# Scaled rows at the head of a spectral block: half-width sums in one bank, rows on two engines, warming products on both sides

## The chip, the cores and the metric

The kernel runs on one core of one Trainium2 chip. A core has a matrix engine (TensorE, "PE" in the profile, with its weight loads listed apart as "PEld"), a vector engine (VectorE, "DVE"), a scalar engine (ScalarE, "ACT"), GpSimd ("POOL") and SyncE ("SP"), which here issues nearly all transfers. Each engine works through its own instructions in the order in which they were written; semaphores tie the engines together. The metric is the device time of the whole program in microseconds.

## The reference, cut to what matters

One block of a network, on x of 2048 rows by 512 columns. A vector c gives six modulation rows; the rows of x are normalised, scaled by one plus a modulation row and shifted; a two-dimensional real FFT, a product with complex weights and the inverse FFT mix the whole matrix; then a second normalisation and a Dense–Mish–Dense layer follow, each part added to x through a gate.

```
mod = (_silu(c) @ w_mod).reshape(c.shape[0], 6, 1, -1)
sa, ca, ga, sb, cb, gb = (mod[:, 0], mod[:, 1], mod[:, 2], mod[:, 3], mod[:, 4], mod[:, 5])
h = _layernorm(x, axis=-1) * (1 + ca) + sa
x = x + ga * _A_ref(h, A_w_r, A_w_i)          # rfft2, times w_r + 1j*w_i, irfft2
h = _layernorm(x, axis=-1) * (1 + cb) + sb
x = x + gb * _B_ref(h, B_w1, B_b1, B_w2)      # Dense, Mish, Dense
```

The change concerns the factor `1 + ca` of the first line of h, and the first microseconds of the program around it.

## The kernel before, in words

The FFT is done as products with constant matrices. x is held in 16 tiles of 128 rows by 512 columns (tile n has every 16th row). The first stage, up to about 49 us, takes each tile through two products: along the columns (`p1_row`, line 269, four products whose stationary operand is the tile's turned x, loaded as `xring` from a second copy of x in memory, and whose moving operand is a block of the constant `kr`), and along the rows (`p1_col`, lines 314 to 316, with the constant `mring`, which `p1_split` makes out of the loaded `mraw` by splitting it into a high and a low part on ACT and POOL).

The scale `1 + ca` is not applied to x. It is put into the constant: `krs = kr * (1 + ca)`, one factor for each partition and each of the four blocks j of 128. So before the first row product can begin, `ca` itself has to be worked out: `scale_sums` (line 325) multiplies the four loaded parts k of `wmc` (256 KB each) with `sc`, which is silu(c): 16 products, each with a 128x128 part of `wmc` as the stationary operand and a column of `sc` spread over the moving columns. All moving columns are alike, so each result column holds the same sums, of which `scale_rows` (line 330, DVE) reads one.

The normalisation is applied late as well. `row_sums` multiplies a matrix of ones with `krs`, and ACT copies the result to `kb` (line 280). For tile n, `norm_sums` (lines 183 and 184, DVE) takes mean and variance, `first_guess` (lines 188 and 189, ACT, a logarithm and an exponential) and `first_scale` (line 196, three small DVE instructions) give one over the standard deviation `rstd`, `p1_mean` (line 284, DVE) subtracts mean times `kb` from the row product's result, `p1_cast` (lines 294 to 300, ACT) multiplies with `rstd` and rounds to the high part, and `p1_low` (line 307, DVE) makes the low part. `p1_col` needs both parts.

Every f32 product appears as two matmul records and two weight loads, so that `scale_sums` has 32 of each. `warm` (line 355) is a series of products of ones with ones whose result nobody reads; they keep PE at work while the first transfers are under way. PSUM banks are taken by `bank(tag)`: tags A, B, C and D, two buffers each.

The order of this stage is written out by hand: the engines' orders are those of the calls in the text (the planner's table further down concerns a later stage). SP's queue begins with `sc`, the four parts of `wmc` and `kr`, and goes on with x, turned x and `mraw`, tile by tile.

Of the kernel before, what the change touches and what calls it, by code (L numbers as in the profile page):

```python
# [7 lines left out]
F32 = mybir.dt.float32  # L8
F32R = mybir.dt.float32r
AF = mybir.ActivationFunctionType  # L10
ALU = mybir.AluOpType

P = 128
# [70 lines left out]
def tile_spectral_block(ctx: ExitStack, tc: tile.TileContext, x_d, w1_d, b1_d, w2_d,  # L84
                        c_d, xt_d, wm_d, wq_d, wz_d, kr_d, km_d, kc_d, ki_d, kf_d, kv_d, kw_d, kp_d, out_d):
    nc = tc.nc
# [4 lines left out]
    small = ctx.enter_context(tc.tile_pool(name="small", bufs=4))  # L91
# [21 lines left out]
    def bank(tag):  # L113
        return psum.tile([P, 512], F32, name="bank", tag=tag)
# [8 lines left out]
    def buf(tag, dt=F32):  # L123
        if tag in "ty":
            uses[tag] = uses.get(tag, 1) + 1
            return wide(tag)[:, uses[tag] % 2]
        return work.tile([P, 512], dt, name="buf", tag=tag)

    def plain(t):
        return t.bitcast(F32)  # L130

    x = base.tile([P, N2, D], F32, name="x")
    sc = base.tile([P, 4], F32, name="sc")
# [6 lines left out]
    krs = modr[:, 0].rearrange("p (j e) -> p j e", j=4)  # L140
# [11 lines left out]
    wmc = big.tile([P, 4, 512], F32, name="wmc", tag="cr")  # L152
# [8 lines left out]
    kr = pw.tile([P, 4, P], F32, name="kr")  # L161
# [6 lines left out]
    def scale_spread():  # L168
        ps = bank("D")
        for k in range(4):  # L170
            nc.tensor.matmul(ps[:, k * P:(k + 1) * P], sc[:, k:k + 1].to_broadcast([P, P]), ident,
                             start=True, stop=True)
        st["scb"] = ps
# [7 lines left out]
    def norm_sums(n):  # L181
        t = small.tile([P, 6], F32, name="st")
        nc.vector.bn_stats(t, x[:, n, :])
        nc.vector.bn_aggr(mv[:, n, :], t)
# [6 lines left out]
    def norm_refine(lo, hi, sign, r=None):  # L191
        r = rstd[:, lo:hi] if r is None else r
        t = small.tile([P, 4], F32, name="ve")[:, 0:hi - lo]
        for out, a, one, op in ((t, mv[:, lo:hi, 1], EPS, ALU.add), (t, t, -0.5 * sign, ALU.mult),
                                (rstd[:, lo:hi], t, 1.5 * sign, ALU.add)):
            nc.vector.scalar_tensor_tensor(out, a, one, r, op0=op, op1=ALU.mult)

    def first_guess(lo, hi):
        st["r", lo] = r = bank("D")[:, 0:hi - lo]
        norm_guess(lo, hi, r)  # L200

    def first_scale(lo, hi):
        norm_refine(lo, hi, -1, st.pop(("r", lo)))
# [27 lines left out]
    def load_m(n):  # L231
        nc.sync.dma_start(mraw[:, n, :], km_d[:, n, :])

    def load_x(n):
        nc.sync.dma_start(x[:, n:n + 1, :], xv[:, n:n + 1, :])

    def load_xt(n):
        t = xring[:, n % 8]
        nc.sync.dma_start(t, xt_d[n])
        st["xt", n] = t  # L240

    def load_all(n):
        load_xt(n)
        load_x(n)
        load_m(n)
# [13 lines left out]
    def p1_split(n):  # L259
        m = mt(n)  # L260
        nc.scalar.copy(m[:, 0, 0:256], mraw[:, n, :])
        nc.gpsimd.tensor_tensor(m[:, 1, 0:256], mraw[:, n, :], plain(m[:, 0, 0:256]), op=ALU.subtract)
        nc.gpsimd.tensor_scalar(m[:, :, 256:384], plain(m[:, :, 128:256]), -1.0, 0.0,
                                op0=ALU.mult, op1=ALU.add)

    def row_products(pg, data):
        pgv = pg.rearrange("p (c d q) -> p d c q", c=2, d=4)
        for j in range(4):
            nc.tensor.matmul(pgv[:, j], data(j), krs[:, j, :].rearrange("p (c q) -> p c q", c=2),  # L269
                             start=True, stop=True)  # L270

    def p1_row(n):
        xt = st.pop(("xt", n))
        st["pg", n] = pg = bank("AB"[n % 2])
        row_products(pg, lambda j: xt[:, j, :])

    def row_sums():
        ps = bank("D")
        row_products(ps, lambda j: ones)
        nc.scalar.copy(kb, ps)  # L280

    def p1_mean(n):
        c = st.pop(("pg", n))
        nc.vector.scalar_tensor_tensor(c, kb, mv[:, n, 0:1], c, op0=ALU.mult, op1=ALU.subtract)
        st["c", n] = c

    def p1_cast(n):
        c = st["c", n]
        one = rstd[:, n:n + 1]
        gh, gl = buf("g1", F32R), buf("g2", F32R)  # L290
        if n in POOL_LOW:
            g = buf("t")
            if n == 1:
                nc.scalar.activation(gh, c, AF.Copy, scale=one)
            nc.scalar.activation(g, c, AF.Copy, scale=one)
            if n > 1:
                nc.scalar.copy(gh, g)
            nc.gpsimd.tensor_tensor(gl, g, plain(gh), op=ALU.subtract)
        else:
            nc.scalar.activation(gh, c, AF.Copy, scale=one)  # L300
        st["g", n] = gh, gl
# [17 lines left out]
    def p1_save(n):  # L319
        nc.scalar.copy(a_sb[:, :, n, :], st.pop(("pa", n)).rearrange("p (e q) -> p q e", e=8))  # L320

    def scale_sums(ks, ps):
        for k in ks:
            for j in range(4):
                nc.tensor.matmul(ps[j][:, 0:P], wmc[:, k, j * P:(j + 1) * P], sc[:, k:k + 1].to_broadcast([P, P]),  # L325
                                 start=(k == 0), stop=(k == 3))

    def scale_rows(ps):
        for j in range(4):
            nc.vector.scalar_tensor_tensor(krs[:, j, :], kr[:, j, :], ps[j][:, 0:1], kr[:, j, :],  # L330
                                           op0=ALU.mult, op1=ALU.add)

    def shift_sum(k):
        mod_column(wms[:, k, :], cols[:, 0, 0, k:k + 1], 128.0, bank("D"))
# [17 lines left out]
    def warm(count, tag="B"):  # L352
        ps = bank(tag)
        for _ in range(count):
            nc.tensor.matmul(ps[:, 0:P], ones, ones, start=True, stop=True)

    with tc.manual_schedule():
        nc.sync.dma_start(sc, c_d.rearrange("b (p k) -> p (b k)", k=4))
        nc.scalar.preload_act_table_set("natural_log_exp_and_others")
        for k in range(4):  # L360
            nc.sync.dma_start(wmc[:, k, :], wm_d[1, k])
        nc.sync.dma_start(kr, kr_d)
        load_x(0)
        load_xt(0)
        nc.sync.dma_start(ident, kp_d)
        load_xt(1)
        load_m(0)
        for n in range(1, 8):
            load_x(n)
            if n < 7:  # L370
                load_xt(n + 1)
            load_m(n)
        nc.vector.memset(ones, 1.0)
        nc.vector.memset(eps, EPS)
        nc.vector.memset(b1n[:, NF - 1:NF], 0.0)
        sg = small.tile([P, 4], F32, name="sg")
        nc.scalar.activation(sg, sc, AF.Exp, scale=-1.0)
        nc.vector.tensor_scalar(sg, sg, 1.0, None, op0=ALU.add)
        nc.vector.reciprocal(sg, sg)
        nc.vector.tensor_tensor(sc, sc, sg, op=ALU.mult)  # L380
        warm(6)
        cps = [bank(t) for t in "CCBB"]
        for k in range(4):
            scale_sums((k,), cps)
        scale_rows(cps)
        row_sums()
        norm_sums(0)
        first_guess(0, 1)
        first_scale(0, 1)
        p1_split(0)  # L390
        p1_row(0)
        load_all(8)
        p1_row(1)
        load_all(9)
        scale_spread()
        p1_mean(0)
        p1_cast(0)
        norm_sums(1)
        first_guess(1, 2)
        p1_split(1)  # L400
        nc.scalar.copy(scb, st.pop("scb"))
        p1_low(0)
        p1_mean(1)
        first_scale(1, 2)
        p1_split(2)
        p1_cast(1)
        norm_sums(2)
        for n in range(N2):
            if n >= 1 and n != 2:
                p1_save(n - 1)  # L410
            if n + 2 < N2:
                p1_row(n + 2)
                if n == 2:
                    p1_col(1, range(2, 3))
                    p1_save(1)
                if n + 10 < N2:
                    load_all(n + 10)
                if n == 4:
                    nc.sync.dma_start(wms, wm_d[0].rearrange("k p e -> p k e"))
                if n == 6:  # L420
                    load_rest()
            if 1 <= n and n + 1 < N2:
                p1_mean(n + 1)
                if n % 2:
                    first_scale(n + 1, n + 3)
                p1_cast(n + 1)
            for i in range(n + 2 + (n > 5), min(n + 3 + (n > 4), N2)) if n else ():
                p1_split(i)
            if n:
                p1_low(n)  # L430
            p1_col(n, range(2) if n == 1 else range(3))
            if n + 3 < N2:
                norm_sums(n + 3)
                if n % 2 == 0:
                    first_guess(n + 2, n + 4)
            if 11 <= n < 15:
                shift_sum(n - 11)
        p1_save(N2 - 1)
        shift_rows()
# [846 lines left out]
    start = {}  # L1286
# [232 lines left out]
```

## Time and profile before

| what | value |
| --- | --- |
| median of 3 runs | 367.63 us (367.40 to 367.93) |
| the profiled execution | 368.36 us, of which its span 366.6 us |
| PE busy | 358.6 us (98% of the span) |
| DVE busy | 302.5 us (83%) |
| ACT busy | 266.9 us (73%) |
| POOL busy | 78.3 us (21%) |
| share of the chain that ended last | PE 84%, ACT 5%, DVE 4%, DMA 2% |

Times in rows of the profile count from the start of the span. A row of the timeline has start, duration, engine, line, operation, output and inputs, shapes and a count; in brackets stands the engine's idle time before it with what ended it. A row with a count above one is a group, and its duration reaches from the first start to the last end. Matmul records overlap: the time from one start to the next is less than the duration of one record.

### The profile page before, as it was taken

How to read it: one execution, taken by the hardware profiler on the slowest of the kernel's cores; microseconds unless marked ns; L12 is line 12 of the kernel's file. 1: busy time of each engine (PE TensorE's matmuls, PEld its weight loads, DVE VectorE, ACT ScalarE, POOL GpSimd, SP SyncE). 2: the span in 40 equal slices, each digit the busy share in tenths (PEclk: the TensorE clock that was granted, in tenths of full speed). 3: DMA queues.
4: the chain of work that ended last, by engine and by line, in shares of the span. 5: the costliest groups of instructions: out<-in, count | busy, mean ns of one | idle time of the engine just before them, and what ended most of it. 6: DMA issues, size and time to landing. Idle time of an engine off the chain costs nothing.

```text
span 366.6 us, 7820 instructions
## 1 busy us (share of the span) xinstructions
PE 358.6 (98%) x2666; PEld 333.9 (91%) x2666; DVE 302.5 (83%) x752; ACT 266.9 (73%) x601; POOL 78.3 (21%) x126
## 2 busy tenths in 40 slices
PE   8999999998999999999999999999999999999994
PEld 8999977777999998798999999999999999999994
DVE  1898968888889799998994777998759977887995
ACT  1798879996799999998773878766577753555650
POOL 0588738786011001100002101004100000000000
PEclk9999999999999999999999999999999999999998
DMA  7999997678498776899888877786989678863133
GB/s 254 383 349 377 331 373 250 219 185 305 142 327 254 236 256 230 278 306 322 248 225 292 276 236 200 207 276 206 281 301 243 215 229 266 227 219 62 59 57 115
DMA packets 54343, 89.96 MB, mean 245 GB/s; under 512 B 7552, under 2 KB 20960, under 8 KB 54048
## 3 DMA queue, kind: packets, MB, share of 16 engines
q1 hardware_dynamic: 49728, 74.65, 62.0%
q0 software_dynamic: 2416, 7.87, 9.0%
q10 hardware_dynamic: 2160, 6.95, 6.0%
q8 instruction: 21, 0.34, 0.4%
q14 instruction: 18, 0.15, 0.1%
HBM read 68.21 MB, written 17.57 MB: 234 GB/s over the span
## 4 chain that ended last, share of the span: by engine, by line
PE 84%; ACT 5%; DVE 4%; DMA 2%; POOL 1%; issue 1%; ACTq 1%; SPq 0%; DVEq 0%; POOLq 0%
PE bank L1091 25%; PE bank L991 22%; PE bank L974 6%; PE bank L269 4%; PE bank L869 4%; PE bank L859 3%; PE bank L860 3%; PE bank L1037 3%; PE bank L314 3%; PE bank L1087 3%; DMA hT<-in_B_w_dram 2%; PE bank L1103 2%; PE bank L316 1%; PE bank L315 1%; PE bank L325 1%
## 5 line engine op out<-in xcount | busy, mean ns | idle before, releaser
L991 PE MATMUL bank<-hT,wr 128*128 128x256 f32 x360 | 51.6, 283 | 0.0
L991 PEld LDWEIGHTS bank<-hT,wr 128*128 128x128 f32 x360 | 47.3, 191 | 0.6
L991 PE MATMUL bank<-hB,wr 128*128 128x256 f32 x318 | 46.6, 285 | 0.0
L991 PEld LDWEIGHTS bank<-hB,wr 128*128 128x128 f32 x318 | 41.9, 191 | 0.9
L1143 POOL DMA_DIRECT2D x<-modr x7 | 6.3, 898 | 140.5 <-DVE modr L1142 84.7
L1091 PE MATMUL bank<-w2a,ah 128*128 128x256 f32 x161 | 35.1, 283 | 0.0
L917 DVE TENSOR_TENSOR al<-buf,ah 128x512 fp32r<-128x512 f32 (+1 forms) x45 | 30.1, 668 | 5.7 <-ACT ah L916 4.7
L1091 PE MATMUL bank<-w2b,ah 128*128 128x256 f32 x147 | 32.2, 283 | 0.0
L916 ACT CAST ah<-buf 128x512 fp32r<-128x512 f32 (+1 forms) x45 | 27.0, 602 | 4.5 <-DVE buf L1061 2.6
L1091 PEld LDWEIGHTS bank<-w2a,ah 128*128 128x128 f32 x161 | 27.0, 191 | 0.4
L859 PE MATMUL bank<-kc,d 128*128 128x128 f32 x128 | 24.9, 276 | 0.5 <-ACT d L452 0.5
L1091 PEld LDWEIGHTS bank<-w2b,ah 128*128 128x128 f32 x147 | 24.9, 191 | 0.3
L860 PE MATMUL bank<-kc,d 128*128 128x128 f32 x128 | 24.8, 275 | 0.0
L974 PE MATMUL bank<-hB,wr 128*128 128x512 f32 x96 | 24.4, 393 | 0.0
L1091 PE MATMUL bank<-w,ah 128*128 128x256 f32 x112 | 21.5, 284 | 0.0
L314 PE MATMUL bank<-buf,mring 128*128 128x512 f32 x48 | 20.6, 430 | 0.2 <-DVE buf L307 0.2
L974 PEld LDWEIGHTS bank<-hB,wr 128*128 128x128 f32 x96 | 17.3, 189 | 3.1
L859 PEld LDWEIGHTS bank<-kc,d 128*128 128x128 f32 x128 | 19.4, 192 | 0.7 <-ACT d L452 0.7
L860 PEld LDWEIGHTS bank<-kc,d 128*128 128x128 f32 x128 | 19.5, 192 | 0.0
L1091 PEld LDWEIGHTS bank<-w,ah 128*128 128x128 f32 x112 | 17.7, 191 | 0.6
L608 PEld LDWEIGHTS bank<-kv,a_sb 128*128 128x128 f32 x126 | 15.5, 192 | 2.8 <-issue 2.2
L788 POOL DMA_DIRECT2D turned<-x x16 | 8.9, 568 | 42.1 <-DVE x L782 42.1
(310 smaller groups left out, 1098.2 us busy)
## 6 DMA issues: line engine op xcount, KB each, us to landing
wr<-w_S SPq DMA_DIRECT2D x60, 256.0 KB, 4.0
wr<-w_A SPq DMA_DIRECT2D x45, 256.0 KB, 3.8
w_S<-hT SPq DMA_DIRECT2D x20, 256.0 KB, 2.9
x<-in_A_x_dram SPq DMA_DIRECT2D x16, 256.0 KB, 4.7
xring<-in_x_t_dram SPq DMA_DIRECT2D x16, 256.0 KB, 4.6
w_A<-wr SPq DMA_DIRECT2D x15, 256.0 KB, 3.1
x<-modr POOLq DMA_DIRECT2D x7, 512.0 KB, 5.5
out_dram<-x SPq DMA_DIRECT2D x7, 512.0 KB, 3.8
```

What stands on the lines that cost most here:

```text
L269: nc.tensor.matmul(pgv[:, j], data(j), krs[:, j, :].rearrange("p (c q) -> p c q", c=2), start=True, stop=True)
L314: nc.tensor.matmul(pa, m[:, a, 0:128], g, start=(i == 0), stop=False)
L608: nc.tensor.matmul(pd[:, i * P:(i + 1) * P], y[:, i * P:(i + 1) * P], kv[:, 0:128], start=True, stop=True)
L859: nc.tensor.matmul(o, dj[:, 0:128], kc[0][:, n, :], start=True, stop=False)
L860: nc.tensor.matmul(o, dj[:, 64:192], kc[1][:, n, :], start=False, stop=True)
L869: nc.tensor.matmul(px[:, j * P:(j + 1) * P], e[:, j * P:(j + 1) * P], kiv[:, j, :], start=True, stop=True)
L916: nc.scalar.copy(h, r)
L917: nc.vector.tensor_tensor(l, r, plain(h), op=ALU.subtract)
L974: nc.tensor.matmul(ups[i, t, f], ring[t, a][:, p, b, :], sides[int(a[2]) - 1][:, :, q, b, :], start=(a[2] == "1" and b == 0 and n == 0), s ...
L991: nc.tensor.matmul(o, w[:, p, k, :], h[:, q, k, :], start=(first and n == 0), stop=(last and n == 5), skip_group_check=True)
L1037: nc.tensor.matmul(ups[i, 0][:FL], w1s[:, p, u, :], sides[u // 2][:, :, q, u % 2, :], start=(u == 0 and p + q == 0), stop=(u == 3 and p == ...
L1091: nc.tensor.matmul(out_ps[b][n][:, 256 * half:256 * half + 256], a[p][:, e], w2[t][q][:, r], start=(t == 1 and half == 0 and i == 0), stop ...
```

## The change

`scale_sums` takes one part k at a time and writes all four blocks j into one PSUM bank (columns 0, 128, 256 and 384 on) in place of four banks. Parts 0 and 1 are multiplied with 128 moving columns, parts 2 and 3 with 64. The flag that starts an accumulation stands at the first product of the bank alone.

`scale_rows` first reads the four sums as one strided row and adds 1 (DVE, 128x4), and then scales the four blocks of `kr`, blocks 0 and 2 on DVE and 1 and 3 on ACT. Before, DVE did all four, each straight from PSUM as `kr * ca + kr`.

`warm(6)` becomes `warm(7)`, and a `warm(4)` follows the sums. The row product of tile 0 moves ahead of `row_sums`. `first_scale(0, 1)` moves from before the splitting of `mraw` to behind `p1_mean(0)`. On SP's queue the turned x of tile 0 goes ahead of x of tile 0, `mraw` of tile 0 ahead of the turned x of tile 1, and that ahead of `ident`.

```diff
-    def scale_sums(ks, ps):
-        for k in ks:
-            for j in range(4):
-                nc.tensor.matmul(ps[j][:, 0:P], wmc[:, k, j * P:(j + 1) * P], sc[:, k:k + 1].to_broadcast([P, P]),
-                                 start=(k == 0), stop=(k == 3))
+    def scale_sums(k, ps):
+        for j in range(4):
+            w = 64 if k > 1 else P
+            nc.tensor.matmul(ps[:, P * j:P * j + w], wmc[:, k, j * P:(j + 1) * P], sc[:, k:k + 1].to_broadcast([P, w]),
+                             start=(k == 0 and j == 0), stop=(k == 3), skip_group_check=True)
 
     def scale_rows(ps):
-        for j in range(4):
-            nc.vector.scalar_tensor_tensor(krs[:, j, :], kr[:, j, :], ps[j][:, 0:1], kr[:, j, :],
-                                           op0=ALU.mult, op1=ALU.add)
+        one = small.tile([P, 4], F32, name="one")
+        nc.vector.tensor_scalar(one, ps[:, 0:512:128], 1.0, None, op0=ALU.add)
+        for j in range(0, 4, 2):
+            nc.vector.tensor_scalar(krs[:, j, :], kr[:, j, :], one[:, j:j + 1], None, op0=ALU.mult)
+            nc.scalar.activation(krs[:, j + 1, :], kr[:, j + 1, :], AF.Copy, scale=one[:, j + 1:j + 2])
...
         nc.sync.dma_start(kr, kr_d)
+        load_xt(0)
         load_x(0)
-        load_xt(0)
+        load_m(0)
+        load_xt(1)
         nc.sync.dma_start(ident, kp_d)
-        load_xt(1)
-        load_m(0)
...
-        warm(6)
-        cps = [bank(t) for t in "CCBB"]
+        warm(7)
+        cps = bank("C")
         for k in range(4):
-            scale_sums((k,), cps)
+            scale_sums(k, cps)
+        warm(4)
         scale_rows(cps)
+        p1_row(0)
         row_sums()
         norm_sums(0)
         first_guess(0, 1)
-        first_scale(0, 1)
         p1_split(0)
-        p1_row(0)
         load_all(8)
         p1_row(1)
         load_all(9)
         scale_spread()
         p1_mean(0)
+        first_scale(0, 1)
         p1_cast(0)
```

PE, the head of the program before (`modr,ones` is `row_sums`, `modr,xring` the row product of a tile, line 171 a spreading of `sc` that is needed later, line 314 the start of tile 0's `p1_col`; the count is of products):

```order
L355 MATMUL bank<-ones 128x128 x6
L325 MATMUL bank<-sc,wmc 128x128 x16
L269 MATMUL bank<-modr,ones 128x2x64 x4
L269 MATMUL bank<-modr,xring 128x2x64 x8
L171 MATMUL bank<-ident,sc 128x128 x4
L269 MATMUL bank<-modr,xring 128x2x64 x4
L314 MATMUL bank<-buf,mring 128x512
```

The same place of PE in the changed kernel:

```order
L357 MATMUL bank<-ones 128x128 x7
L325 MATMUL bank<-sc,wmc 128x128 x8
L325 MATMUL bank<-sc,wmc 128x64 x8
L357 MATMUL bank<-ones 128x128 x4
L269 MATMUL bank<-modr,xring 128x2x64 x4
L269 MATMUL bank<-modr,ones 128x2x64 x4
L269 MATMUL bank<-modr,xring 128x2x64 x4
L171 MATMUL bank<-ident,sc 128x128 x4
L269 MATMUL bank<-modr,xring 128x2x64 x4
L314 MATMUL bank<-buf,mring 128x512
```

Between the last of the sums and `row_sums` there was nothing; now four warming products and tile 0's row product stand there.

DVE from the scaling of the rows on, before (`BN_STATS` and `BN_AGGR` are `norm_sums`, of tile 0 and then of tile 1):

```order
L330 SCALAR_TENSOR_TENSOR modr<-kr,bank 128x128 x4
L183 BN_STATS st<-x 128x6
L184 BN_AGGR mv<-st 128x2
L196 SCALAR_TENSOR_TENSOR ve<-mv,bank 128x1
L196 SCALAR_TENSOR_TENSOR ve<-ve,bank 128x1
L196 SCALAR_TENSOR_TENSOR rstd<-ve,bank 128x1
L284 SCALAR_TENSOR_TENSOR bank<-modr,mv,bank 128x512
L183 BN_STATS st<-x 128x6
L184 BN_AGGR mv<-st 128x2
L307 SCALAR_TENSOR_TENSOR buf<-bank,rstd,buf 128x512
```

The same place of DVE in the changed kernel:

```order
L330 TENSOR_SCALAR one<-bank 128x4
L332 TENSOR_SCALAR modr<-kr,one 128x128 x2
L183 BN_STATS st<-x 128x6
L184 BN_AGGR mv<-st 128x2
L284 SCALAR_TENSOR_TENSOR bank<-modr,mv,bank 128x512
L196 SCALAR_TENSOR_TENSOR ve<-mv,bank 128x1
L196 SCALAR_TENSOR_TENSOR ve<-ve,bank 128x1
L196 SCALAR_TENSOR_TENSOR rstd<-ve,bank 128x1
L183 BN_STATS st<-x 128x6
L184 BN_AGGR mv<-st 128x2
L307 SCALAR_TENSOR_TENSOR buf<-bank,rstd,buf 128x512
```

The three small instructions of `first_scale` stood ahead of `p1_mean` (line 284) and now stand behind it; from the second `BN_STATS` on the two orders agree.

## The prediction

> **What bounds the kernel now.** I read the page's first lines, then the chain that ended last in its first 24 us, then busy time by stretches, and at last the timeline of the head, instruction by instruction. Busy time by stretch (us, then PE, PE's loads, DVE, ACT, POOL, granted clock, DMA share, GB/s):
>
> ```profile
> span 366.6 us, 7820 instructions
> 11.30:20.00 8.70, 8.52 (x62) 7.62 (x60) 8.42 (x22) 6.91 (x16) 5.63 (x9) 1.00 1.06 379
> 20.00:48.00 28.00, 27.99 (x203) 26.00 (x202) 25.87 (x68) 23.69 (x55) 22.05 (x30) 1.00 1.02 348
> ```
>
> From 20 us on PE has no gap; whatever moves its start there moves the end of the stage. From 11.3 to 20 us DVE is the full one, 8.42 of 8.70. The chain (start, duration, work) says the same:
>
> ```profile
> 4.21 4.53 PE bank L325 x32
> 8.74 2.86 PE bank L269 x24
> ...
> 13.44 0.75 DVE bank L284
> ...
> 18.74 0.75 DVE buf L307
> ...
> 19.54 0.50 PE bank L314
> ```
>
> It runs through PE's sums and row products, goes over to DVE at 13.44, and returns to PE at 19.54 by way of line 307, the low part that `p1_col` of tile 2 waits for. So two things count: when DVE gets its first `p1_mean`, and how much it does after that. Here is the head:
>
> ```profile
> 1.04 2.93 PE L355 MATMUL bank<-ones 128*128 128x128 f32 x12 [1.04 <-DVE b1n L375]
> 4.21 4.53 PE L325 MATMUL bank<-sc,wmc 128*128 128x128 f32 x32 [0.24 <-DMA wmc<-in_w_mod_dram]
> 8.11 1.16 DVE L330 SCALAR_TENSOR_TENSOR modr<-kr,bank 128x128 f32<-128x128 f32 x4 [4.87 <-PE bank L325]
> 8.58 1.23 PE L269 MATMUL bank<-modr,ones 128*128 128x128 f32 x8
> 9.65 1.95 PE L269 MATMUL bank<-modr,xring 128*128 128x128 f32 x16
> 9.85 0.58 ACT L280 COPY modr<-bank 128x512 f32<-128x512 f32 x1 [7.22 <-PE bank L269]
> 10.33 0.27 ACT L188 ACTIVATE bank<-mv,eps 128x1 f32<-128x1 f32 x1
> 10.63 0.16 ACT L189 ACTIVATE bank<-bank 128x1 f32<-128x1 f32 x1
> 10.82 0.15 DVE L196 SCALAR_TENSOR_TENSOR ve<-mv,bank 128x1 f32<-128x1 f32 x1 [0.73 <-ACT bank L189]
> 11.01 0.16 DVE L196 SCALAR_TENSOR_TENSOR ve<-ve,bank 128x1 f32<-128x1 f32 x1
> 11.20 0.16 DVE L196 SCALAR_TENSOR_TENSOR rstd<-ve,bank 128x1 f32<-128x1 f32 x1
> 11.27 0.75 DVE L284 SCALAR_TENSOR_TENSOR bank<-modr,mv,bank 128x512 f32<-128x512 f32 x1
> 11.44 1.06 PE L171 MATMUL bank<-ident,sc 128*128 128x128 f32 x8
> 11.93 0.69 DVE L183 BATCH_NORM_STATS2 st<-x 128x6 f32<-128x512 f32 x1
> 12.33 1.06 PE L269 MATMUL bank<-modr,xring 128*128 128x128 f32 x8
> 13.14 0.48 PE L314 MATMUL bank<-buf,mring 128*128 128x512 f32 x1
> ```
>
> The order of events is: sums on PE, `krs` on DVE, `row_sums` on PE, its copy `kb` on ACT, and behind that copy, on ACT's queue, the logarithm and exponential that `first_scale` waits for. DVE sits idle until 10.82, and from there it is full until 19.5. Eight records of 128 columns take 0.89 us (11.44 to 12.33), 0.111 each.
>
> **The change part by part.**
>
> *64 columns in parts 2 and 3.* This is 8 products, 16 records. If the columns set the pace, a record falls from 0.111 to about 0.056 us and the sums end 0.87 us sooner; if the weight load sets it, nothing is won. No row has 64 columns, so the loads have to speak (the first three rows are from the timeline, the second and third of it in windows of their own; the last gives shortest, median and longest):
>
> ```profile
> 57.39 0.09 PEld L476 LDWEIGHTS bank<-kf,early 128*1 128x1 f32 x2 [0.17 <-issue]
> 57.75 0.19 PEld L479 LDWEIGHTS bank<-kf,early 128*128 128x128 f32 x1 [0.28 <-issue]
> 57.86 0.19 PEld L479 LDWEIGHTS bank<-kf,early 128*128 128x128 f32 x1
> L479 PE MATMUL bank<-kf,early x2: 299/352/404, 57.8 to 58.0; 128*128 128x160 f32 x2
> ```
>
> Both instances had PE to themselves. Two loads of one column lie inside 0.09 us. With 128 columns the second load begins 0.11 us after the first, and the first product, issued with the first load, takes 404 ns where the other takes 299: it waits 0.105 us for its weights. The load takes some 0.11 us by its 128 columns, as long as the product over 128 moving columns that now covers it. A half-width product still needs a whole load: `wmc` keeps its 128x128 parts. I take 0.109 in place of 0.111, 0.03 us in all, and keep 0.87 as the other end. [...]
>
> *`warm(7)`.* Two more records, at the slow pace of the start (12 in 2.93 us, about 0.21 each), end where PE waited for `wmc` until 4.21 anyway. Cost 0 while the first part lands at 4.1; if it landed earlier, up to 0.2. It can win at most the 0.1 us by which the first record behind a gap is longer. I take 0.
>
> *`warm(4)`.* Eight records at 0.111, 0.89 us, between the sums and everything else on PE. Part of this covers the scaling of the rows, which PE before had hidden differently: each block of `krs` was used as soon as it was there, at the price of a stretch to 1.07 us (8.58 to 9.65) for eight records of `row_sums` instead of 0.89. So 0.89 comes on and 0.18 goes.
>
> *One bank, rows on two engines.* All four sums must now be complete before the first row is scaled. The price, by the nearest rows:
>
> ```profile
> L378 DVE TENSOR_SCALAR sg<-sg 128x4 f32<-128x4 f32 x1 | 0.2, 170 | 1.7 <-ACT sg L377 1.7
> L456 DVE TENSOR_SCALAR d<-bank 128x128 f32<-128x128 f32 x9 | 2.6, 284 | 0.5 <-ACT d L452 0.5
> L454 ACT ACTIVATE d<-bank 128x128 f32<-128x128 f32 x8 | 2.4, 297 | 0.0
> ```
>
> 0.17 for the addition, then two rows of at most 0.3 on each engine in parallel: the first is there about 0.55 us after the sums' result, the last about 0.85. PE comes for the first at 0.89 and for the last 0.67 later, so `warm(4)` hides all of it; without it PE would wait some 0.6. Cost 0.
>
> *Tile 0's row product ahead of `row_sums`.* `kb` comes eight records later, 0.89 us. For PE alone it is an exchange.
>
> *Transfers.* The same transfers in another order:
>
> ```profile
> 4.00 0.43 SPq L239 DMA_DIRECT2D xring<-in_x_t_dram  x1
> 4.96 0.43 SPq L239 DMA_DIRECT2D xring<-in_x_t_dram  x1
> xring<-in_x_t_dram SPq DMA_DIRECT2D x1, 256.0 KB, 4.8
> ```
>
> The turned x of tile 0, issued at 4.00, landed 4.8 us later, at 8.8; one place of 256 KB earlier, about 0.7, it lands near 8.1, x in its old place near 8.8, and the turned x of tile 1, issued at 4.96, at 9.8 instead of 9.7. PE asks for them at 9.4 and 11.2, DVE for x at about 9.2. Hidden; from x of tile 1 on nothing moves.
>
> *`first_scale` behind `p1_mean`.* Before, its 0.45 us (10.82 to 11.27) lay in front of `p1_mean` in time that DVE spent waiting. Now it costs its whole length behind `p1_mean`: 0.19 + 0.19 + 0.07 = 0.45 of DVE. The logarithm still stands behind the copy of `kb` on ACT, so moving it spares nothing at the front.
>
> **The sum.** Sums end for PE at 8.58 - 0.03 = 8.55; `warm(4)` to 9.44; tile 0 to 10.33; `row_sums` to 11.22, its result 0.16 later (before: 9.81 against 9.65), 11.38. The copy starts 0.04 later and takes 0.58: 12.00. `p1_mean` at 12.04 (before 11.27). The next DVE instruction follows 0.66 later (11.27 to 11.93), so `first_scale` stands at 12.70 to 13.15. Its exponential is done in time: the logarithm comes 0.48 after the copy's start, the exponential 0.30 later, its result 0.19 after that, 12.39. `BN_STATS` of tile 1 starts at 13.15, before 11.93: **1.22 us later**. The work that follows it on DVE is the same, and DVE had no idle time there, so line 307 of tile 2 comes 1.2 later, and with it PE's full stretch from 19.54 on. PE itself is through its row products at about 13.9 and finds tile 0's cast not done until 14.0, so DVE and ACT, not PE, keep the lead. The profiled execution was 368.36 us by its clock, 1.8 over its span and 0.7 over the median of the runs; the difference is set on the median: 367.63 + 1.2 = 368.8.
>
> **The rivals.**
>
> *Half the columns, half the time.* For it: no row excludes it. Against it: the loads above. Then the sums end 0.84 us earlier than I take, and the sum is 1.22 - 0.84, about +0.4: 368.0, within what a measurement of this kernel can tell from no change (0.2%, 0.74 us). A clock that comes to full speed earlier goes the same way: between 4.5 and 5.5 us six records start, between 6 and 7 eleven.
>
> ```profile
> 4.50:5.50 1.00, 1.00 (x6) 1.00 (x6) 0.00 (x0) 0.00 (x0) 0.00 (x0) 1.00 0.95 352
> 6.00:7.00 1.00, 1.00 (x11) 1.00 (x10) 0.00 (x0) 0.00 (x0) 0.00 (x0) 1.00 1.04 385
> wmc<-in_w_mod_dram SPq DMA_DIRECT2D x1, 256.0 KB, 4.2
> ```
>
> If the gap before 4.21 had held the faster pace back, closing it could win up to eight times 0.1; but the last part of `wmc`, issued at 2.58, lands 4.2 us later, at 6.8, and eight records of 0.109 behind it end no earlier than 7.7, again +0.4.
>
> *Not slower: the delay is swallowed.* Between 11.3 and 20 us PE has idle time. If tile 2's column product is set by PE's own order and not by line 307, PE, which is 0.7 late with its row products, makes that up in its gaps, and the time is about 367.6. It decides if DVE reaches line 307 of tile 2 by 18.8, that is, if 1.2 us of DVE's 8.42 busy microseconds were waits in disguise. The chain speaks against it.
>
> *Worse: the faster pace comes later.* [...] If the change of pace, now near 5.7, slips by 3 us or more, half of that is lost: +2.7 in all, 370.3. [...]
>
> **How the numbers follow.** The forecast, +1.2: 0.66, with a range of its own from 368.4 to 369.3 (0.4 down for a load that is partly hidden or waits that give way, 0.5 up for rows or casts that come late). Half time or early clock, +0.4: 0.18. Swallowed: 0.09. Later pace: 0.07. The range from 367.8 to 369.4 leaves out the last and the greater part of the swallowed case. Slower: nine tenths of the forecast and the worst case, 0.66; the same: the +0.4 case, most of the swallowed one, the forecast's lower tenth, 0.28; faster: 0.06, what is left of the swallowed case together with an early pace.
>
> **What would show it.** In the changed profile: the 64-column rows of line 325 start 0.11 apart; `p1_mean` of tile 0 starts near 12.0 and `BN_STATS` of tile 1 near 13.15; line 307 of tile 2 near 19.95; PE's full stretch from about 20.8. Starts 0.06 apart make the first rival right; `p1_mean` near 12.0 with line 307 at 18.8 the second. The forecast falls if `kb` is there before 11.2.

## The result, and the profile after

The changed kernel takes 369.0 us in the median (368.72 to 369.81, eight runs) against 367.75 us before (367.4 to 368.62, eight runs of the same chip): a ratio of 1.0034, 95% interval 1.0023 to 1.0045. It is slower by 1.25 us; the forecast was 1.2. The interval reaches from 0.85 to 1.65 us, so a hit to 0.05 us is luck; what the runs below can bear out is the working behind it.

The chain that ended last, after the change, from its start to PE's full stretch (start, duration, work):

```profile
4.39 4.62 PE bank L325 x32
9.01 0.95 PE bank L357 x8
9.96 1.80 PE bank L269 x16
...
11.78 0.59 ACT modr L280
...
12.40 0.76 DVE bank L284
...
20.31 0.76 DVE buf L307
...
21.11 0.50 PE bank L314
```

Before, the chain went from PE's row products straight to DVE, at the `p1_mean` of tile 1. Now the copy of `kb` on ACT (line 280) stands between them: that copy has become what the first `p1_mean` (line 284) waits for. The other end of the chain is as it was: line 307 of tile 2, then PE without a gap. The timeline of the same head shows the steps one by one (start, duration, engine, line, work, idle time before and what ended it):

```profile
1.04 3.35 PE L357 MATMUL bank<-ones 128*128 128x128 f32 x14 [1.04 <-DVE b1n L377]
4.19 4.83 PE L325 MATMUL bank<-sc,wmc 128*128 128x128 f32 x32
8.85 1.11 PE L357 MATMUL bank<-ones 128*128 128x128 f32 x8
9.05 0.16 DVE L330 TENSOR_SCALAR one<-bank 128x4 f32<-128x4 f32 x1 [5.84 <-PE bank L325]
9.25 0.48 DVE L332 TENSOR_SCALAR modr<-kr,one 128x128 f32<-128x128 f32 x2
9.80 1.06 PE L269 MATMUL bank<-modr,xring 128*128 128x128 f32 x8
10.69 1.06 PE L269 MATMUL bank<-modr,ones 128*128 128x128 f32 x8
11.78 0.59 ACT L280 COPY modr<-bank 128x512 f32<-128x512 f32 x1 [1.84 <-PE bank L269]
12.40 0.76 DVE L284 SCALAR_TENSOR_TENSOR bank<-modr,mv,bank 128x512 f32<-128x512 f32 x1 [1.85 <-ACT modr L280]
13.52 0.69 DVE L183 BATCH_NORM_STATS2 st<-x 128x6 f32<-128x512 f32 x1
```

From the end of the sums for PE, where its next record starts, to the statistics of tile 1 it was 3.35 us before (8.58 to 11.93) and is 4.67 now (8.85 to 13.52): 1.32 more. The sums themselves ended 0.27 later, because PE went over to its faster pace at 6.58 in this execution and at 5.73 in the one before (read from the starts of single records). Together the statistics are 1.59 later, line 307 of tile 2 is 1.57 later (18.74 to 20.31) and PE's full stretch 1.57 later (19.54 to 21.11).

Busy time by stretch in the changed kernel (PE, PE's loads, DVE, ACT, POOL, granted clock, DMA share, GB/s) shows the same picture as before, later: DVE full up to 21, then PE.

```profile
13.50:21.00 7.50, 7.38 (x49) 6.23 (x47) 7.22 (x21) 6.43 (x15) 5.10 (x9) 1.00 1.03 364
21.00:48.00 27.00, 26.89 (x196) 25.15 (x196) 24.95 (x65) 23.37 (x55) 22.33 (x31) 1.00 1.04 359
```

The two profiled spans differ by only 0.9 us (366.6 and 367.5), since the profiled execution of the kernel before lost time later on, at a place that the change does not touch. There ACT waited for a transfer (timeline of the kernel before):

```profile
95.59 0.71 ACT L739 CAST wr<-hT 128x256 fp32r<-128x256 f32 x2 [1.11 <-DMA hT<-in_B_w_dram]
```

PE waited 0.35 us for ACT behind it, at 97.77; up to there the changed kernel's products start 1.5 us later than these, and from there on 0.97. The same work of ACT after the change (timeline) has no such wait:

```profile
95.86 0.71 ACT L742 CAST wr<-hT 128x256 fp32r<-128x256 f32 x2
```

From the first product behind the stage to the end of the span the kernel before took 317.82 us (48.77 to 366.59) and the changed one 317.24 (50.25 to 367.49). So the head costs 1.5 us in this pair of profiles, and 0.58 of that is offset by one late transfer in one execution. The timed runs, 1.25 us apart, are the measure.

### The profile page after: what moved, and what is told of

Same layout as the page of the kernel before. It is cut to its first block, busy times and chain, and to the rows that moved or that the text cites. A ratio compares the mean times of both kernels' runs of the same rounds, so it can differ in the third digit from the quotient of the medians.

```text
span 367.5 us, 7842 instructions
## 1 busy us (share of the span) xinstructions
PE 360.0 (98%) x2676; PEld 335.5 (91%) x2676; DVE 302.1 (82%) x751; ACT 267.5 (73%) x603; POOL 78.3 (21%) x126
## 4 chain that ended last, share of the span: by engine, by line
PE 90%; DVE 4%; ACT 3%; issue 1%; POOL 0%; ACTq 0%; DVEq 0%
PE bank L1094 25%; PE bank L994 22%; PE bank L977 6%; PE bank L862 4%; PE bank L872 4%; PE bank L863 4%; PE bank L269 3%; PE bank L1040 3%; PE bank L314 3%; PE bank L1090 3%; PE bank L562 3%; PE bank L611 2%; PE bank L542 2%; PE bank L1106 1%; PE bank L315 1%; PE bank L316 1%
```

## The experiments

Ten kernels ran. All compute the whole result: where a product gets fewer moving columns, each column holds the same sum, and line 330 reads one of them. Times are compared with runs of the kernel before on the same chip. Beside the time stands the distance from the end of the sums for PE to the statistics of tile 1, which leaves out when PE's pace changed. (In the changed kernel without `warm(4)` PE waits behind the sums; there they are taken to end 0.11 us after the start of their last record, as elsewhere.) The distance is worth reading, though each comes from one traced execution, because all that follows is constant: from the statistics of tile 1 to the end of the stage it was 36.73 to 36.91 us in every kernel here but the one with eight columns (37.78).

| Kernel | Distance, us | Ratio to before, 95% interval |
|---|---|---|
| before | 3.35 | |
| changed | 4.67 | 1.0034 [1.0023, 1.0045] |
| 64 columns alone | 3.38 | 0.9999 [0.9985, 1.0013] |
| `warm(7)` alone | 3.35 | 1.0008 [0.9990, 1.0027] |
| `first_scale` behind `p1_mean` alone | 3.33 | 1.0008 [0.9994, 1.0023] |
| changed, `row_sums` first again | 4.11 | 1.0010 [0.9996, 1.0024] |
| changed, four banks again, no `warm(4)` | 3.89 | 1.0011 [0.9998, 1.0023] |
| changed, without `warm(4)` | 4.56 | 1.0023 [1.0011, 1.0036] |
| changed, `first_scale` ahead again | 5.37 (two transfers late) | 1.0018 [1.0003, 1.0034] |
| before, 64 columns in all four parts | 4.20 (half at the slow pace) | 1.0065 [1.0034, 1.0096] |
| before, eight columns in all four parts | 4.46 (all at the slow pace) | 1.0078 [1.0049, 1.0107] |
| before, the 1 added on PE, `kb` copied later | 3.00 | 0.9979 [0.9962, 0.9995] |

**64 columns alone.** The kernel before, with

```diff
             for j in range(4):
+                w = 64 if k > 1 else P
-                nc.tensor.matmul(ps[j][:, 0:P], ..., sc[:, k:k + 1].to_broadcast([P, P]),
+                nc.tensor.matmul(ps[j][:, 0:w], ..., sc[:, k:k + 1].to_broadcast([P, w]),
```

> The kernel before, with 64 moving columns in parts 2 and 3 of the sums and nothing else. Theory (the load of 128x128 weights sets the pace): records 0.11 us apart as with 128 columns, row_sums begin within 0.05 us of where they did for the same change of PE's pace, no change in time. Rival (the columns set the pace): records 0.06 apart, row_sums up to 0.87 us earlier, and 0.4 to 0.6 us faster than before, what PE's gaps between 13 and 20 us allow.

Its timeline, PE at the end of the sums:

```profile
6.84 2.00 PE L326 MATMUL bank<-sc,wmc 128*128 128x64 f32 x16 [0.73 <-DMA wmc<-in_w_mod_dram]
8.67 1.26 PE L269 MATMUL bank<-modr,ones 128*128 128x128 f32 x8
```

Sixteen records of 64 columns take from 6.84 to 8.67, 0.114 us each with the longer first one behind the wait; records of 128 columns took 0.111. Half the columns win nothing. There is a second thing: by the starts of single records PE had its full pace from 4.30 here, and the row shows that it then waited 0.73 us for part 2 of `wmc`. An early pace cannot bring the sums forward by much, since the data are not there.

**`first_scale` behind `p1_mean` alone.** The kernel before, with

```diff
         first_guess(0, 1)
-        first_scale(0, 1)
         p1_split(0)
...
         p1_mean(0)
+        first_scale(0, 1)
         p1_cast(0)
```

> The kernel before, with one part of the change alone: first_scale of tile 0 stands behind p1_mean of tile 0. Theory (DVE's chain from p1_mean on sets the end): kb was there at 10.43 and the exponential only at 10.82, so p1_mean moves into the wait and starts near 10.5, first_scale near 11.15, BN_STATS of tile 1 near 11.6 instead of 11.93; 0.35 us faster than before. Reading of the prediction (first_scale behind p1_mean costs its 0.45 us of DVE): 0.45 us slower than before. If DVE's chain does not set the end: no change.

Its timeline:

```profile
9.99 1.95 PE L269 MATMUL bank<-modr,xring 128*128 128x128 f32 x16
10.19 0.58 ACT L280 COPY modr<-bank 128x512 f32<-128x512 f32 x1 [7.60 <-PE bank L269]
11.14 0.75 DVE L284 SCALAR_TENSOR_TENSOR bank<-modr,mv,bank 128x512 f32<-128x512 f32 x1 [0.71 <-ACT bank L189]
12.25 0.69 DVE L183 BATCH_NORM_STATS2 st<-x 128x6 f32<-128x512 f32 x1
```

`p1_mean` comes 2.22 us behind the sums in place of 2.69, 0.47 sooner, and `first_scale` then takes its 0.45 behind it: the distance stays. The 0.35 that I expected as a gain is not there. `kb` was copied at 10.77, yet `p1_mean` began at 11.14. The row names the exponential of line 189, which ended at that moment; but in the changed kernel `p1_mean` starts at 12.40, ahead of the exponential at 12.57, so it does not need it. What fits is tile 0's own row product: its eight records start from 9.99 on, 0.111 apart, and a record lasts about 0.28, so it ends near 11.05. In the order of before, tile 0's product and not `kb` is what `p1_mean` waits for. (In the kernel with eight columns, further down, the row of line 284 names that product.)

**Without `warm(4)`.** The changed kernel, with

```diff
             scale_sums(k, cps)
-        warm(4)
         scale_rows(cps)
```

> The changed kernel without the four warming products behind the sums. Theory: tile 0's row product starts when the first scaled row is there, some 0.4 to 0.5 us after the sums end for PE and not 0.95 us, waits once more for ACT's second row, and ends 0.4 us earlier; kb, p1_mean and line 307 of tile 2 come 0.4 us earlier, and the kernel is 0.4 us faster than the changed one. If the warming products cost their whole 0.89: 0.9 us faster. If they keep the clock up: the gap of half a microsecond brings slow records back (0.2 us apart), and it is slower.

Its timeline:

```profile
8.93 0.16 DVE L330 TENSOR_SCALAR one<-bank 128x4 f32<-128x4 f32 x1 [5.70 <-PE bank L325]
9.47 1.16 PE L269 MATMUL bank<-modr,xring 128*128 128x128 f32 x8 [0.58 <-DVE modr L332]
10.47 1.06 PE L269 MATMUL bank<-modr,ones 128*128 128x128 f32 x8
12.18 0.76 DVE L284 SCALAR_TENSOR_TENSOR bank<-modr,mv,bank 128x512 f32<-128x512 f32 x1 [1.75 <-ACT modr L280]
13.29 0.69 DVE L183 BATCH_NORM_STATS2 st<-x 128x6 f32<-128x512 f32 x1
```

Taking eight records of 0.111 us out of PE's queue spares 0.11 us, not 0.89, and less than the 0.4 that I expected. In their place stand a wait of 0.58 for the first scaled row (an addition, a row, and two handovers between engines) and a stretch of the next eight records to 1.00 us. The cost lies in the form of the scaling, not in the filler: the addition reads all four sums in one instruction, so no row can begin before the last of them is done.

**`row_sums` first again.** The changed kernel, with

```diff
         scale_rows(cps)
-        p1_row(0)
         row_sums()
+        p1_row(0)
```

> The changed kernel with row_sums ahead of tile 0's row product, as before. Theory: kb is there 0.89 us earlier (near 11.4 where it was near 12.4 in the changed kernel's profile), p1_mean with it; the kernel is 0.9 us faster than the changed one and 0.3 us slower than before. If PE's own order sets the end and not kb: no change against the changed kernel, since PE does the same work.

Its timeline:

```profile
8.26 1.11 PE L357 MATMUL bank<-ones 128*128 128x128 f32 x8
9.20 1.06 PE L269 MATMUL bank<-modr,ones 128*128 128x128 f32 x8
10.10 1.95 PE L269 MATMUL bank<-modr,xring 128*128 128x128 f32 x16
10.30 0.58 ACT L280 COPY modr<-bank 128x512 f32<-128x512 f32 x1 [0.95 <-PE bank L269]
11.26 0.76 DVE L284 SCALAR_TENSOR_TENSOR bank<-modr,mv,bank 128x512 f32<-128x512 f32 x1 [1.08 <-ACT bank L189]
12.37 0.69 DVE L183 BATCH_NORM_STATS2 st<-x 128x6 f32<-128x512 f32 x1
```

4.11 in place of 4.67: the order of the two products on PE is worth 0.56, and not the 0.9 that I expected. The copy comes 0.89 sooner (2.04 us behind the sums in place of 2.93), but `p1_mean` only 0.55 (3.00 in place of 3.55), because tile 0's product is then what it waits for: it ends near 11.16 by the same reckoning, and the row again names line 189. What is left to the kernel with `first_scale` moved alone, 4.11 against 3.33, is 0.78: the price of everything that was done to the sums and rows, with `warm(7)` and the order of the loads.

**Four banks again, no `warm(4)`.** The other half alone: the changed kernel with `scale_sums` and `scale_rows` of before (four banks, 128 columns, each row scaled on DVE as its sum is there), so that the order of the products, `first_scale` behind `p1_mean`, `warm(7)` and the order of the loads are what is left of the change.

```diff
-        cps = bank("C")
+        cps = [bank(t) for t in "CCBB"]
         for k in range(4):
-            scale_sums(k, cps)
-        warm(4)
+            scale_sums((k,), cps)
         scale_rows(cps)
         p1_row(0)
```

> The changed kernel with the sums and the scaled rows of before (four banks, 128 columns, four rows on DVE straight from PSUM) and without the warming products behind them; the order of row products, first_scale and transfers stays changed. Theory (waiting for all four sums, the addition and the first row cost PE 0.74 us, which the warming products fill to 0.95; the exchange of row_sums and tile 0's product costs 0.55): tile 0's product begins at the end of the sums, BN_STATS of tile 1 3.9 after it (before 3.35, changed 4.67), and the kernel is 0.5 us slower than before and 0.8 us faster than the changed one. If the order alone were the cause: as slow as the changed kernel.

Its timeline:

```profile
8.91 1.23 PE L269 MATMUL bank<-modr,xring 128*128 128x128 f32 x8
11.69 0.76 DVE L284 SCALAR_TENSOR_TENSOR bank<-modr,mv,bank 128x512 f32<-128x512 f32 x1 [1.27 <-ACT modr L280]
12.80 0.69 DVE L183 BATCH_NORM_STATS2 st<-x 128x6 f32<-128x512 f32 x1
```

3.89, or 0.54 over before. Two halves by two ways, 0.54 to 0.56 and 0.78, make 1.32 to 1.34; the whole is 1.32. The kernel without `warm(4)`, at 4.56, is 0.67 above this one. There, 0.74 us passed on PE from the end of the sums to the start of the first row product, and that product was stretched 0.07 less (1.00 for 1.07): the new form of the scaling accounts for the 0.67, and `warm(4)` adds 0.11. No run separates the one bank from the addition as an instruction of its own or from the sharing of the rows between DVE and ACT.

**`first_scale` ahead again.** The changed kernel, with

```diff
         first_guess(0, 1)
+        first_scale(0, 1)
         p1_split(0)
...
         p1_mean(0)
-        first_scale(0, 1)
```

> The changed kernel with first_scale of tile 0 back ahead of p1_mean. Since the change of PE's pace falls at another moment in every execution, places are counted from the end of the sums on PE. In the changed kernel p1_mean comes 3.55 us and BN_STATS of tile 1 4.67 us after it. Theory (kb is what p1_mean waits for there, and the exponential comes 0.35 us after kb): p1_mean 4.35 and BN_STATS of tile 1 5.0 after the sums, 0.35 us slower than the changed kernel. By the reading that first_scale behind p1_mean costs 0.45 us: 0.45 us faster than the changed kernel.

Its timeline:

```profile
8.31 0.48 DVE L332 TENSOR_SCALAR modr<-kr,one 128x128 f32<-128x128 f32 x2 [0.17 <-DMA kr<-in_kr_dram]
9.56 0.69 DVE L183 BATCH_NORM_STATS2 st<-x 128x6 f32<-128x512 f32 x1 [0.77 <-DMA x<-in_A_x_dram]
11.07 0.59 ACT L280 COPY modr<-bank 128x512 f32<-128x512 f32 x1 [2.07 <-PE bank L269]
12.49 0.75 DVE L284 SCALAR_TENSOR_TENSOR bank<-modr,mv,bank 128x512 f32<-128x512 f32 x1
13.15 0.69 DVE L183 BATCH_NORM_STATS2 st<-x 128x6 f32<-128x512 f32 x1
```

In this execution the full pace came at 4.06 and the sums ended at 7.78, so early that `kr` and `x` were late, and the distance from the sums is not to be compared. From the copy on it is: 2.08 us to the statistics of tile 1 (11.07 to 13.15) against 1.74 in the changed kernel (11.78 to 13.52). In the new order, `first_scale` ahead of `p1_mean` costs 0.34 more than behind it. The timed runs can't separate the two: the intervals overlap, and the ratio, 1.0018, is if anything below the changed kernel's 1.0034. The 0.34 rests on the two traces alone.

**Eight columns, and 64, in all parts.** The kernel before, with

```diff
-                nc.tensor.matmul(ps[j][:, 0:P], ..., sc[:, k:k + 1].to_broadcast([P, P]),
+                nc.tensor.matmul(ps[j][:, 0:8], ..., sc[:, k:k + 1].to_broadcast([P, 8]),
```

> The kernel before, with 8 moving columns in place of 128 in all four parts of the sums. Theory (a load of 128 columns sets the pace): records still 0.11 us apart at the full pace, and not less; at the slow pace 0.16 to 0.21 apart; no change in time beyond 0.2 us. Rival (the columns set the pace): records about 0.03 apart, the sums over soon after the last part of wmc has landed, 0.5 us faster than before. [...]

Timeline there:

```profile
4.12 6.97 PE L325 MATMUL bank<-sc,wmc 128*128 128x8 f32 x32 [0.15 <-DMA wmc<-in_w_mod_dram]
10.94 2.05 PE L269 MATMUL bank<-modr,ones 128*128 128x128 f32 x8
14.74 0.76 DVE L284 SCALAR_TENSOR_TENSOR bank<-modr,mv,bank 128x512 f32<-128x512 f32 x1 [0.20 <-PE bank L269]
```

and the same edit with 64 in place of 8:

> The kernel before, with 64 moving columns in all four parts of the sums. With 8 columns in all parts the full pace came only at 16.5 us. If what counts there is how long columns move through the array: with 64 in all parts the sums' slow stretch keeps the array moving half the time, the full pace comes later than in the profiles with 128 columns in the first two parts (4.0 to 6.7 us), near 8 to 10 us, and the kernel is 1 to 2 us slower than before. If 64 columns are enough: the full pace comes between 4.0 and 6.7 us, records 0.11 apart after it, and the time is that of before.

Busy time by stretch in the kernel with 64:

```profile
5.10:8.40 3.30, 2.71 (x25) 2.58 (x24) 0.00 (x0) 0.00 (x0) 0.00 (x0) 1.00 0.98 333
8.50:11.80 3.30, 3.30 (x17) 3.30 (x17) 1.94 (x6) 0.55 (x2) 0.00 (x0) 0.50 1.05 369
11.90:14.00 2.10, 2.10 (x21) 2.10 (x21) 1.71 (x5) 1.10 (x4) 1.12 (x2) 1.00 0.90 275
```

With eight columns the pace is slow until 16.54, long after the sums: 32 records take 6.82 us, 0.213 each, as slow as records of 128 columns at the start (0.213 each from 1.41 to 3.97 in the changed kernel). So at the slow pace too the moving columns do not set a record's time; the load of 128 columns of weights, which all of them have, fits. With 64 columns everywhere the granted clock falls to 0.50 behind a stretch at full clock, 17 records in 3.30 us where there had been 25 (a window counts those under way at its ends too) in as long a stretch with a wait of 0.58 in it, and returns. That is not what I expected for 64: the full pace came at 5.00, within the usual range (4.00 to 6.69), and was then lost again. For eight columns the forecast of no change was wrong: the full pace came at 16.54, where in the ten kernels compared at the end it came by 6.69. Fewer moving columns win nothing and cost time, 0.65% with 64 and 0.78% with eight, and the two traces show the pace as what is lost. Among executions it varies (367.49 to 372.37 and 367.87 to 372.27), and the profile with 64 columns, of an execution of 369.2 us, is of a milder one; what the slower ones lost is not traced. The split of half the parts in the change under study did not do this.

**`warm(7)` alone.** The kernel before, with

```diff
-        warm(6)
+        warm(7)
```

> The kernel before with seven warming products ahead of the sums in place of six, the change's part alone. Theory: the seventh ends where PE waited for the first part of wmc; the full pace comes at any moment between 4.0 and 6.7 us as it did with six, and the time is that of before within 0.2%. Rival (the gap ahead of the sums holds the full pace back): it comes at 4.5 us or sooner, and the kernel is 0.3 us or more faster than before.

The distance is the same to 0.01 us, the time within the interval. The two records cost nothing.

**The 1 added on PE, `kb` copied later.** What the runs point to: keep each row's start on its own sum, and take work off the path. The kernel before, with four products of ones by 1/128 opening the four sums in place of four of the six warming products, which brings the 1 of `1 + scale` in ahead of time, and the copy of `kb` behind the logarithm and exponential on ACT.

```diff
...
-                                 start=(k == 0), stop=(k == 3))
+                                 start=False, stop=(k == 3))
+
+    def scale_ones(ps):
+        for j in range(4):
+            nc.tensor.matmul(ps[j][:, 0:P], ones, inv.to_broadcast([P, P]), start=True, stop=False)
 
     def scale_rows(ps):
         for j in range(4):
-            nc.vector.scalar_tensor_tensor(krs[:, j, :], kr[:, j, :], ps[j][:, 0:1], kr[:, j, :],
-                                           op0=ALU.mult, op1=ALU.add)
+            nc.vector.tensor_scalar(krs[:, j, :], kr[:, j, :], ps[j][:, 0:1], None, op0=ALU.mult)
...
-        warm(6)
+        warm(2)
         cps = [bank(t) for t in "CCBB"]
+        scale_ones(cps)
...
-        row_sums()
+        sums = row_sums()
         norm_sums(0)
         first_guess(0, 1)
+        nc.scalar.copy(kb, sums)
         first_scale(0, 1)
```

> A version of the kernel before that follows from the theory. Four of the six warming products add the one into the four sums (ones times 1/128), so that a row is kr times a sum, a shorter DVE instruction without a second pass over kr; and ACT does the logarithm and exponential of tile 0 ahead of the copy of kb. Theory: row_sums are no longer stretched (0.89 in place of 1.07 us), first_scale is done before tile 0's product is there, p1_mean begins about 2.1 us after the sums (before 2.69) and BN_STATS of tile 1 2.8 to 2.9 after them (before 3.35); 0.4 to 0.5 us faster than before. If DVE's chain does not set the end: no change.

Its timeline:

```profile
8.32 0.97 DVE L335 TENSOR_SCALAR modr<-kr,bank 128x128 f32<-128x128 f32 x4 [5.12 <-PE bank L326]
8.79 1.05 PE L270 MATMUL bank<-modr,ones 128*128 128x128 f32 x8
10.62 0.16 DVE L197 SCALAR_TENSOR_TENSOR ve<-mv,bank 128x1 f32<-128x1 f32 x1 [0.52 <-ACT bank L190]
11.13 0.75 DVE L285 SCALAR_TENSOR_TENSOR bank<-modr,mv,bank 128x512 f32<-128x512 f32 x1
11.80 0.69 DVE L184 BATCH_NORM_STATS2 st<-x 128x6 f32<-128x512 f32 x1
```

The four rows take 0.97 us where they took 1.16, so `row_sums` no longer waits for them (8.79 to the next product at 9.69 is 0.90 for eight records, where before it was 1.07), and `first_scale` starts 1.83 behind the sums in place of 2.24. The distance is 3.00, 0.35 less than before and 0.1 to 0.2 more than I expected: the copy of `kb`, now behind the logarithm and the exponential, ended at 11.10, and `p1_mean` followed it at 11.13, 2.34 behind the sums and not 2.1. The time is 367.46 us against 368.16, a ratio of 0.9979 with 0.9962 to 0.9995: a little faster than the kernel before, and so than the changed one. The 0.35 us of the head are 0.1%, which lies inside that interval; the rest of the 0.21% is not explained by the profile. The two edits were not run apart.

## Why the prediction was right, and where its working was not

- *The bound.* Right. `BN_STATS` of tile 1, line 307 of tile 2, PE's full stretch and the end of the stage moved together, by 1.59, 1.57, 1.57 and 1.48 us.
- *64 columns, set by the load, 0.03 us.* Right: 0.114 apart in the kernel with them alone, nothing won. Of the two ends weighed there, the pace of the loads is borne out (0.11 us for 128 columns of weights at line 479, measured 0.111 to 0.114 a record), the halved record of 0.056 is not, for products that each bring their own weights. The 0.109 that the prediction took has no row behind it; behind the longer first record they started 0.112 apart, and the gain of 0.03 was not there (3.38 against 3.35).
- *`warm(7)`, nothing.* Right, by the kernel with it alone. The sums ended at 8.85, not 8.55, because the full pace came later in that execution; in the kernel with `warm(7)` alone, where it came at 6.57, they ended at 8.90.
- *`warm(4)` +0.89 - 0.18, one bank and rows on two engines nothing.* The sum of 0.71 is close to the 0.78 measured, but it was put down to the wrong edit. `warm(4)` itself costs 0.11, and its eight records took 0.95 (8.85 to 9.80), not 0.89, which is most of the difference. The price is that of the gathered scaling: all four sums, then the addition, then the first row, before PE goes on. The prediction had that as a side remark ("without it PE would wait some 0.6"; measured 0.58), and booked it at nothing because the filler covers it.
- *Tile 0's product ahead of `row_sums`, `kb` 0.89 later.* Right: the copy starts 2.93 behind the sums with this order and 2.04 with the other.
- *`first_scale`: "moving it spares nothing at the front", 0.45 lost.* This step is wrong. Before the change, `p1_mean` could have started 0.47 sooner, when tile 0's product was done; `first_scale` stood in its way, and its 0.45 was on the path already. Moved alone, it costs and wins nothing (3.33 against 3.35). In the new order moving it wins 0.34. The loss belongs to the exchange of the products: `kb` and not tile 0's product became the last thing that `p1_mean` waits for.
- *Why the number held all the same.* The sum did not follow that sentence. It puts `p1_mean` 0.04 behind the end of the copy, where before it came 0.84 behind it (10.43 to 11.27). So it spares 0.80 at the front and gives 0.45 back behind: 0.35 won, and 0.34 was measured. With 0.89 for the exchange that makes 0.54 for the new order, and 0.54 to 0.56 was measured. The steps of the sum held, and the price put on `first_scale` beside it did not.
- *Two readings of the head.* "DVE sits idle until 10.82" leaves out its work from 8.11 to 10.09, on the rows and tile 0's statistics; its wait was 0.73 us. The six and eleven records said to start between 4.5 and 5.5 and between 6 and 7 us include those under way at the ends of the windows; five and nine start there. Neither enters the sum.
- *Transfers hidden.* Right: no wait for `kr`, `x` or the turned x stands in the changed kernel's head. They have little to spare: with the sums done at 7.78, `kr` and `x` were late.
- *The sum.* Distances forecast: 3.49 us from the sums to `p1_mean`, 4.60 to the statistics; measured 3.55 and 4.67. The absolute places, 12.04, 13.15, 19.95 and 20.8, came out at 12.40, 13.52, 20.31 and 21.11, of which 0.3 is the later end of the sums and 0.06 the longer `warm(4)`.
- *The rivals.* Half time fell with the kernel with 64 columns alone. Swallowed fell too: its point was line 307 of tile 2 by 18.8, and it stood at 20.31. A later pace was there in small, 0.27 us in this execution, but it comes just as late in kernels with full columns (6.69 with `first_scale` moved alone), so the columns of this change are not shown to be its cause. The slip of 3 us behind the +2.7 was a supposition that no run shows: the full pace came 0.85 us later here than before (6.58 against 5.73), and 10.81 later with eight columns. That fewer columns can cost the pace is what the two kernels that go further show (slow until 16.54 with eight, slow again from 8.41 to 11.82 with 64).

## What to carry to other kernels

Before an edit is costed, ask of the instruction that leads the path what it waits for last, and what second last: delaying the producer that comes second last costs only what goes beyond its distance to the last (here 0.89 less 0.35). An instruction on the same engine that must be done either way costs its length ahead of the waiting one as well as behind it (3.35 and 3.33 here), unless its own input comes later than what the waiting one needs; then it belongs behind (0.34 here). Four results gathered into one wait start the next work when the last is done, and a filler that covers the wait hides it from the idle times, not from the time of the run (a wait of 0.58 us without the filler, and 0.11 us spared by leaving it out). Narrower moving operands saved nothing on TensorE here, where each product brings its own 128 columns of weights (0.112 us apart with 64 moving columns, 0.111 with 128).

## What the hardware showed that was not expected

The pace of TensorE changed at three moments 3.41 us apart in the kernel with 64 columns everywhere: to full at 5.00, to half at 8.41, to full at 11.82 (by the starts of single records; the granted clock reads 1.00 from 5.10 to 8.40, 0.50 from 8.42 to 11.80 and 1.00 again from 11.83). What sets these moments the traces do not show. From 5.00 to 8.41 PE's sequence of records was as dense as at full pace elsewhere (0.112 us apart, 0.111 in the kernel before), but for one wait of 0.58 us, and the clock was still halved behind it. With 128 columns in the first half of the sums and a wait of 0.73 us, the kernel with 64 columns in parts 2 and 3 alone kept its pace (0.114 us apart from 6.84 to 8.67). With eight columns there was no wait inside the sums, and the full pace came late all the same (16.54). So moving columns count, as far as one traced execution of each kernel shows; whether the wait of 0.58 had a share in the halving was not tried.

The moment of the first change was 4.00 to 6.69 us from the start in ten kernels that start alike (first record at 1.04): 5.73 before, 6.58 after, 4.00 with `row_sums` first. It is worth less than it looks. Where it came at 4.00 the sums ended at 8.26, and where it came at 6.69 at 8.93: PE waited for the last part of `wmc` instead. The timeline of the kernel with 4.00:

```profile
7.32 1.10 PE L325 MATMUL bank<-sc,wmc 128*128 128x64 f32 x8 [0.33 <-DMA wmc<-in_w_mod_dram]
```

The clock column of a stretch does not show the slow pace at the start: it reads 1.00 also from 4 to 6.5 us, where records start 0.21 us apart. How many records fall into a stretch tells it. Busy time by stretch, changed kernel (PE alone):

```profile
4.20:6.50 2.30, 2.30 (x12) 1.00 0.84 291
6.60:8.80 2.20, 2.20 (x22) 1.00 0.98 335
```
